# Other widths of query units in the second and third batch of a sketched-attention and expert-mixing kernel

## The chip, the cores and the metric

The kernel runs on one core of one Trainium2 chip. The time is the device time of one execution in microseconds (us); the median of four executions before the change is 489.26 us (489.24 to 489.73). TensorE multiplies matrices (PE in the profile; PEld are its weight loads), VectorE (DVE), ScalarE (ACT) and GpSimd (POOL) work on elements, and SyncE (SP) issues the DMA transfers. Each engine runs its instructions in the order in which the program emits them and waits on semaphores for the others.

## The reference

Two blocks follow each other. The first is attention without a softmax: queries and keys go through a product of two small projections (`phi`, 8 x 8 = 64 features), the keys of a batch are summed into one matrix per head, and each query row is multiplied with it and divided by its sum. The second mixes four experts: each is a two-layer network with a ReLU, weighted per row by a normalised gate.

```python
# q, k, v: (4, 4, 1088, 32); S1, S2: (8, 32)
def phi(x):
    a = np.einsum('rd,bhsd->bhsr', S1, x)
    b = np.einsum('rd,bhsd->bhsr', S2, x)
    return np.einsum('bhsi,bhsj->bhsij', a, b).reshape(*x.shape[:-1], 64)
q_p, k_p = phi(q), phi(k)
kv = np.einsum('bhsf,bhsd->bhfd', k_p, v)
z = np.sum(k_p, axis=2)
num = np.einsum('bhsf,bhfd->bhsd', q_p, kv)
den = np.einsum('bhsf,bhf->bhs', q_p, z)[..., None] + 1e-06
x = (num / den).transpose(0, 2, 1, 3).reshape(4352, 128)
# w1: (4, 128, 1024), w2: (4, 1024, 128)
p = domain_probs / (domain_probs.sum(-1, keepdims=True) + 1e-09)
out = sum(p[:, e:e+1] * (np.maximum(x @ w1[e], 0) @ w2[e]) for e in range(4))
```

## The kernel before

The 4352 rows of `x` are the columns of one SBUF tile `xT` (128 x 4352). Two streams of work share the engines.

The expert stream cuts the columns into eleven chunks, `CHUNKS = [128, 448, 512, 512, 512, 512, 512, 512, 320, 256, 128]`, counted here from 0. Chunk 3 begins at column 1088, chunk 4 at 1600, chunk 5 at 2112, chunk 6 at 2624, chunk 7 at 3136, chunk 8 at 3648. Each chunk takes 16 steps (`NQ`), one for each pair of 128-wide blocks of the hidden layer; "step 2.13" below is step 13 of chunk 2. A step runs `first(i)`: two groups of matmuls `h<-xT,w_sb` (j = 0 and 1), each followed by a ReLU on ACT (L807) and, on DVE, by one or two rectify-and-subtract operations (L778, three a step), and after each group a call of `work()`. Then it runs `second(i - 2)`: the matmuls `o<-hid` of the step two before. The `h` results rotate through three PSUM banks, so a group waits for the DVE and ACT readers of the group three before it. Every fourth step an expert is complete, and `gather` and `gather_rest` add it up on ACT and POOL.

The attention stream is a generator, `front()`, which makes `xT` batch by batch (1088 columns each): first `keys(b)`, then one `queries(b, c, n)` for each unit of `n` columns listed in `UNITS[b]`. It is cut into pieces by `yield`: 19 for the keys of a batch, 20 for a unit. Pieces of the keys: three transposes `kT`, three projections `kf`, eight products `kp` (DVE, L383), two empty ones, two `kv` sums on PE, one `kvx`. Pieces of a unit: the transpose `qT` (L480), two empty ones, the projection (`qc`, PE, `f<-qT,sq`), the shuffles and the addition `qf`, `qf`, `qb` (L629 to L634), twice `qa` (L639) with two products `qp` (L493), three empty ones, the attention matmuls (`den<-kvx,qp`), the reciprocal `rc` (L565, L570), the quotient `xs` (L574), and at last the transpose `y` (L583) with the stores: four DMAs put `y` into a DRAM buffer `xd` (L601) and a fifth brings it back as columns of `xT` (L609). Five DMAs a unit, all issued by SP.

How wide the unit is decides its tiles: `blocks(n)` gives ceil and floor of n/128. A unit of up to three tiles uses one PSUM bank, `den`; a fourth tile goes into a second bank, `num`, and `rc` and `xs` then have one instruction more each. Where the two numbers differ (320, 448), `qT` takes two transposes in place of one.

How many pieces a step carries is planned. `needed[m]` counts the pieces up to the end of the unit that completes the columns of chunk `m`. In each step the loop sets

```python
rate = CHUNKS[m] / NQ * max([0] + [(needed[c] + (8 if c > 1 else 4) - done[0]) / (START[c] - gone) for c in range(m + 1, NC)])
```

where `done[0]` counts pieces emitted and `gone` the columns already begun: the steepest line from now to eight pieces after each later chunk's need. Each `work()` adds half of `rate` to a credit and emits a piece for each whole credit. Pieces go into the engines' queues at that place: the DVE work of a piece stands between the L778 operations of the expert stream.

On SP the transfers stand in program order: the stores and the load of each unit, `load_gate(m + 1)` at step m.5, the output of chunk m - 1 at about step m.7, and `load_batch(b + 1)` (L93, L99, L104) after the keys of batch b.

Of the kernel before, what the change touches and what calls it, by code (L numbers as in the profile page):

```python
# [23 lines left out]
def kernel(  # L24
# [25 lines left out]
    P = 128  # L50
# [11 lines left out]
    CW = 512  # L62
    GE = 160
    LA = 2
    UNITS = [[P, 448, 512]] + [[384, 384, 320]] * 2 + [[384, 320, 384]]

    CHUNKS = [P, 448, 512] + [512] * 5 + [320, 256, P]
    NC = len(CHUNKS)
    START = [sum(CHUNKS[:m]) for m in range(NC)]
    assert all(sum(u) == S for u in UNITS) and sum(CHUNKS) == B * S  # L70

# [594 lines left out]
    def start():  # L666


        b, n = 0, UNITS[0][0]
        kf = []  # L670
# [39 lines left out]

        n1 = UNITS[b][1]
        qT = apool.tile([P, QW], F32, tag="qT2", name="qT2")
# [14 lines left out]
    def front():  # L727
        for b in range(B):
# [4 lines left out]
            c = 0  # L733
            for n in UNITS[b]:
                if b or c:
# [218 lines left out]

    needed, columns, count = [0] * NC, UNITS[0][0], 0
    for b in range(B):
        count += 19 if b else 0
        for n in UNITS[b] if b else UNITS[0][1:]:
            count, columns = count + (20 if count else 18), columns + n
# [76 lines left out]
```

## Time and profile before

| | |
|---|---|
| median of four executions | 489.26 us |
| the profiled execution | 489.73 us, of which the span is 487.9 us |
| PE busy | 482.2 us (99%) |
| DVE busy | 319.7 us (66%) |
| ACT busy | 247.0 us (51%) |
| POOL busy | 230.5 us (47%) |
| granted TensorE clock | 1.0 |

A line of the timeline begins with the start in us from the beginning of the span and the duration in us of a run of alike instructions; then come engine, line, operation, output and inputs, shapes and the number of instructions, and in brackets the idle time of the engine before it with what ended it. A `MATMUL` line counts instructions of which each 32-bit product takes two. A line of the view by stretches begins with the stretch; behind it stand its length and each engine's busy time in it with the number of instructions.

Chunk 1 begins at about 29 us, chunk 2 at 78.27, chunk 3 at 133.42, chunk 4 at 190.57, chunk 5 at 244.80, chunk 6 at 300.24, chunk 7 at 354.89, chunk 8 at 407.87 and chunk 9 at 442.22 us: the starts of the first `h` matmul of each.

### The profile page before, as it was taken

How to read it: one execution, taken by the hardware profiler on the slowest of the kernel's cores; microseconds unless marked ns; L12 is line 12 of the kernel's file. 1: busy time of each engine (PE TensorE's matmuls, PEld its weight loads, DVE VectorE, ACT ScalarE, POOL GpSimd, SP SyncE). 2: the span in 40 equal slices, each digit the busy share in tenths (PEclk: the TensorE clock that was granted, in tenths of full speed). 3: DMA queues.
4: the chain of work that ended last, by engine and by line, in shares of the span. 5: the costliest groups of instructions: out<-in, count | busy, mean ns of one | idle time of the engine just before them, and what ended most of it. 6: DMA issues, size and time to landing. Idle time of an engine off the chain costs nothing.

```text
span 487.9 us, 11354 instructions
## 1 busy us (share of the span) xinstructions
PE 482.2 (99%) x4543; PEld 367.5 (75%) x4543; DVE 319.7 (66%) x754; ACT 247.0 (51%) x496; POOL 230.5 (47%) x269
## 2 busy tenths in 40 slices
PE   8999999999999999999999999999999999999997
PEld 5966767677667777777777777777777777999996
DVE  6858685868766757768675674576574676665642
ACT  4354553445454634545455554545455455566751
POOL 5172653516345444424555354334555346565570
PEclk9999999999999999999999999999999999999999
DMA  8890230040102520041102200021101200120000
GB/s 241 256 305 5 90 93 2 12 126 1 35 1 91 129 55 1 1 118 24 34 0 87 50 2 2 1 86 24 34 0 56 50 1 0 45 53 6 15 3 18
DMA packets 37588, 26.25 MB, mean 54 GB/s; under 512 B 26016, under 2 KB 34592, under 8 KB 37024
## 3 DMA queue, kind: packets, MB, share of 16 engines
q1 hardware_dynamic: 37520, 25.53, 18.9%
q8 instruction: 36, 0.59, 0.5%
q14 instruction: 16, 0.13, 0.1%
q10 hardware_dynamic: 16, 0.00, 0.0%
HBM read 21.28 MB, written 4.24 MB: 52 GB/s over the span
## 4 chain that ended last, share of the span: by engine, by line
PE 72%; ACT 0%; DVE 0%; issue 0%
PE h L194 37%; PE o L194 31%; PE f L194 2%; PE den L194 2%; ACT sh L926 0%; PE num L194 0%; DVE end L846 0%
## 5 line engine op out<-in xcount | busy, mean ns | idle before, releaser
L194 PE MATMUL h<-xT,w_sb 128*64 128x512 f32 (+5 forms) x1432 | 299.4, 490 | 0.5 <-DVE hid L778 0.3
L778 DVE SCALAR_TENSOR_TENSOR hid<-h,hid 128x256 f32<-128x256 f32 (+6 forms) x432 | 203.9, 472 | 146.1 <-ACT hid L807 137.3
L807 ACT ACTIVATE hid<-h 128x512 f32<-128x512 f32 (+3 forms) x288 | 158.5, 551 | 194.3 <-PE h L194 154.3
L194 PE MATMUL o<-hid,w2s 128*64 128x256 f32 (+3 forms) x1152 | 222.9, 355 | 0.0
L194 PEld LDWEIGHTS h<-xT,w_sb 128*64 128x64 f32 x1432 | 147.9, 137 | 50.2 <-issue 5.8
L194 PE MATMUL o<-hid,w_sb 128*64 128x256 f32 (+3 forms) x864 | 183.8, 355 | 0.0
L194 PEld LDWEIGHTS o<-hid,w2s 128*64 128x64 f32 x1152 | 132.1, 137 | 29.2 <-issue 1.0
L922 POOL TENSOR_TENSOR ev<-yz,sh 64x256 f32<-64x256 f32 (+3 forms) x72 | 48.1, 668 | 161.7 <-ACT sh L925 159.0
L194 PEld LDWEIGHTS o<-hid,w_sb 128*64 128x64 f32 x864 | 100.7, 137 | 21.6 <-issue 3.4
L910 POOL TENSOR_TENSOR yz<-ev 128x512 f32<-128x512 f32 (+3 forms) x36 | 42.6, 1183 | 59.3 <-ACT ev L913 59.2
L922 POOL TENSOR_TENSOR ct<-ev 128x512 f32<-128x512 f32 (+3 forms) x36 | 42.4, 1178 | 2.8
L922 POOL TENSOR_TENSOR total<-total,ct 128x512 f32<-128x512 f32 (+3 forms) x27 | 32.3, 1195 | 2.1
L922 POOL TENSOR_TENSOR ct<-ct,gate 128x512 f32<-128x512 f32 (+3 forms) x27 | 32.2, 1191 | 2.1
L493 DVE TENSOR_TENSOR qp<-qa,qb 64x384 f32<-64x384 f32 (+3 forms) x44 | 30.4, 691 | 1.1
L912 ACT COPY ev<-o 128x512 f32<-128x512 f32 (+3 forms) x36 | 19.4, 539 | 11.9 <-PE o L194 11.5
L194 PE MATMUL o<-w_sb,hid 128*64 128x128 f32 x256 | 21.3, 274 | 0.0
L913 ACT COPY ev<-o 128x512 f32<-128x512 f32 (+3 forms) x36 | 19.4, 539 | 2.3 <-PE o L194 0.4
L194 PEld LDWEIGHTS o<-w_sb,hid 128*64 128x64 f32 x256 | 16.9, 137 | 1.8 <-issue 0.9
L799 ACT ACTIVATE hid<-h 128x256 f32<-128x256 f32 x24 | 8.8, 385 | 18.2 <-PE h L194 17.8
L383 DVE TENSOR_TENSOR kp<-fs 128x256 f32<-128x256 f32 (+1 forms) x24 | 15.0, 633 | 0.1
L194 PEld LDWEIGHTS den<-kvx,qp 128*64 128x64 f32 x264 | 13.0, 137 | 2.4 <-issue 0.5
L925 ACT COPY sh<-yz 64x256 f32<-64x256 f32 (+3 forms) x36 | 13.7, 380 | 1.7 <-POOL yz L910 0.8
(126 smaller groups left out, 239.5 us busy)
## 6 DMA issues: line engine op xcount, KB each, us to landing
w_sb<-in_moe_w_dram SPq DMA_DIRECT2D x8, 512.0 KB, 7.7
gate<-gates SPq DMA_DIRECT2D x4, 1024.0 KB, 4.7
kn<-in_k_dram SPq DMA_DIRECT2D x4, 544.0 KB, 4.3
vn<-in_v_dram SPq DMA_DIRECT2D x16, 128.0 KB, 4.5
gate<-gates SPq DMA_DIRECT2D x2, 896.0 KB, 4.5
qn<-in_q_dram SPq DMA_DIRECT2D x3, 544.0 KB, 5.7
xd<-y SPq DMA_DIRECT2D x26, 48.0 KB, 1.7
out_dram<-ob SPq DMA_DIRECT2D x16, 64.0 KB, 2.1
```

The lines of the kernel that those rows point to most:

```text
L194: nc.tensor.matmul(out(s), weights(s), moving(s), **flags)
L383: eng.tensor_tensor(out=_ap(kps[b], 0, P, 256 * t0 + P * p + 64 * x, [[256, n], [32, 2], [R, 4], [1, R]]), in0=_ap(src, 0, P, off + 4 * x, ...
L493: nc.vector.tensor_tensor(out=qp[p][64 * x : 64 * x + 64, 0:n], in0=qa[64 * p : 64 * p + 64, 0:n], in1=qb[64 * p : 64 * p + 64, 0:n], op=A ...
L778: nc.vector.scalar_tensor_tensor(out=out, in0=src, scalar=0.0, in1=in1, op0=ALU.max, op1=ALU.subtract)
L799: nc.scalar.activation(hd[:, 0 : 2 * n], hp[:, 0 : 2 * n], ACTF.Relu)
L807: nc.scalar.activation(hd[:, n * j : n * j + n], hp[:, 0:n], ACTF.Relu)
L910: add = lambda out, in0, in1, op=ALU.add: nc.gpsimd.tensor_tensor(out=out, in0=in0, in1=in1, op=op)
L912: nc.scalar.copy(_ap(ev, 0, P, 0, [[2 * w, 2], [1, w]]), _ap(a0, 0, P, 0, two))
L913: nc.scalar.copy(_ap(ev, 0, P, w, [[2 * w, 2], [1, w]]), _ap(a1, 0, P, 0, two))
L922: add = lambda out, in0, in1, op=ALU.add: nc.gpsimd.tensor_tensor(out=out, in0=in0, in1=in1, op=op)
L925: nc.scalar.copy(sh[HP:P, 0:w], yz[0:HP, 0, 0:w])
```

## The change

One constant is different. Batch 0 and batch 3 keep their units; in batch 1 the units 384, 384, 320 become 512, 320, 256, in batch 2 they become 448, 512, 128.

```diff
-    UNITS = [[P, 448, 512]] + [[384, 384, 320]] * 2 + [[384, 320, 384]]
+    UNITS = [[P, 448, 512], [512, 320, 256], [448, 512, P], [384, 320, 384]]
```

The ends of the units in columns of `xT` move from 1472, 1856, 2176 to 1600, 1920, 2176 in batch 1 and from 2560, 2944, 3264 to 2624, 3136, 3264 in batch 2. The number of pieces in all stays 275. With the rule for `needed` this gives, for chunks 0 to 10:

```
before  0 18 38 97 117 176 196 235 255 275 275
after   0 18 38 77 117 156 176 235 255 275 275
```

## The prediction

> **What bounds the kernel now.** I read the busy times and the chain that ended last, then the view by stretches for the places where PE is not full, then the timeline there, SP's lines included.
>
> ```profile
> PE 482.2 (99%) x4543; PEld 367.5 (75%) x4543; DVE 319.7 (66%) x754; ACT 247.0 (51%) x496; POOL 230.5 (47%) x269
> ...
> PE 72%; ACT 0%; DVE 0%; issue 0%
> ```
>
> ```profile
> 48.00:60.00 12.00, 12.00 (x135) 9.50 (x135) 8.06 (x21) 6.38 (x13) 6.55 (x8) 1.00 0.27 84
> 60.00:72.00 12.00, 11.71 (x92) 7.53 (x90) 9.21 (x18) 7.41 (x16) 7.36 (x9) 1.00 0.34 102
> ...
> 132.00:144.00 12.00, 11.79 (x82) 6.96 (x80) 9.23 (x23) 5.84 (x11) 7.05 (x6) 1.00 0.04 14
> 144.00:156.00 12.00, 12.00 (x108) 8.80 (x106) 7.59 (x17) 6.49 (x12) 6.54 (x6) 1.00 0.07 16
> ```
>
> PE (the first pair of numbers behind the comma) is full. Behind the start-up (24 us) only two of the twelve-us stretches ahead of the last one are short of 12.00, so the change can win only what these two lack, and can lose by making a third. "Busy" is generous, because the modelled end of a matmul hides a short gap; I take the size of a stall from the spacing of starts. Undisturbed, two steps of a 512 chunk take 6.45 us (the chain has h groups at 187.51 and 193.96), alternately 3.27 and 3.19.
>
> ```profile
> 67.24 1.05 DVE L383 TENSOR_TENSOR kp<-fs 128x256 f32<-128x256 f32 x1
> ...
> 69.42 1.45 DVE L383 TENSOR_TENSOR kp<-fs 128x320 f32<-128x320 f32 x1
> ...
> 70.79 0.38 DVE L778 SCALAR_TENSOR_TENSOR hid<-h,hid 128x224 f32<-128x224 f32 x1
> ...
> 71.22 0.97 PE L194 MATMUL h<-xT,w_sb 128*64 128x448 f32 x4 [0.29 <-DVE hid L778]
> ```
>
> The first stall, in step 1.14. The h group at 71.22 waits for the L778 that ends at 71.17, and that one stood behind products of batch 1's keys of 1.05 and 1.45 us, where the unhindered ones take 0.56; POOL worked from 65.3 to 72.8 almost without a pause. Steps 1.13 and 1.14 begin at 67.00 and 69.67, step 1.15 at 73.16: 6.16 us for a pair that takes 5.66 one pair earlier (61.34 to 67.00), 0.50 too much. Steps 1.14 and 1.15 together (69.67 to 78.27) take 8.60, less 5.66, less 2.10 for the 72 `kv` matmuls (steps 3.11 and 3.12, which carry as many, take 8.55 and not 6.45): 0.84. First stall: 0.50 to 0.84.
>
> ```profile
> 124.94 0.57 DVE L583 STREAM_TRANSPOSE y<-xs 128x384 f32<-128x384 f32 x1
> ```
>
> ```profile
> 125.54 1.73 SPq L601 DMA_DIRECT2D xd<-y  x4
> 130.83 0.34 SPq L609 DMA_DIRECT2D xT<-xd  x1
> ...
> 133.42 1.94 PE L194 MATMUL h<-xT,w_sb 128*64 128x512 f32 x8 [0.21 <-ACT sh L926]
> ...
> 341.10 1.74 SPq L601 DMA_DIRECT2D xd<-y  x4
> 344.21 0.34 SPq L609 DMA_DIRECT2D xT<-xd  x1
> ```
>
> The second stall is the beginning of chunk 3. The bracket names an ACT copy, which this matmul doesn't read; what it reads and what comes last is `xT`, whose columns from 1472 on belong to the unit stored at 125.54. Their load was issued only at 130.83, and with the 2.3 us that such a load takes it lands at 133.1. Step 2.15 begins at 129.60 and carries no matmul of the other stream, so chunk 3 should begin at 132.87: 0.55 us. From store to use this transfer took 7.9 us; at 341.10 the load came 2.2 us sooner behind the stores.
>
> **The change part by part.** PE: the tiles per batch are 3+3+3 before, 4+3+2 and 4+4+1 after, nine each; the projections cover 1088 columns a batch either way. The instruction counts of PE, ACT, POOL and SP stay. Nothing, and it needs no cover.
>
> DVE: a 384 unit costs, by its rows, qT 0.56, qf 0.59 + 0.55, qb 0.59, qa 2 x 0.585, qp 4 x 0.75, rc 0.39, xs 0.55, y 0.57: 8.0 us. A 512 unit: 0.67, 0.74 + 0.68, 0.73, 2 x 0.73, 4 x 0.78, rc 0.57, xs 0.55 + 0.28, y 0.71: 9.5. A 320 unit 6.9. For 256 and 128 the shuffles have no row; those for 512 and 320 (0.735, 0.515) fall 0.22 over 192 columns, which puts them near 0.44 and 0.29. With the 128x256 and 128x128 rows of the rest these units come to 5.8 and 3.8, a 448 unit to 8.8. Batch 1: 22.9 before, 22.2 after; batch 2: 22.9 and 22.1. The six extra instructions (three rc at 0.16, three xs at 0.28) are in that. DVE is idle a third of the span, so its total is worth nothing; its places count.
>
> The plan: with `needed` of chunk 3 at 77 and not 97, the steepest line is flatter. Following the loop, pieces per step go from 2.6 to 2.1 in chunk 1, 3.0 to 2.4 in chunk 2, 2.5 to 2.4 in chunks 3 and 4, and from 1.85 up to 2.4 in 5 and 6; chunk 7 keeps 1.5.
>
> First stall. The eight `kp` move from steps 1.11-1.13 to 1.12-2.0 and get four steps, not 2.75. A 448 step lasts 2.83 us, of which L778 takes 1.4, so 1.25 steps more give DVE 1.8 us, over twice the stall. But POOL's stretch now meets about four of the eight. At 1.1 us each (blocked ones took 0.88, 1.05, 1.45) steps 1.12 to 1.14 need some 1.5 us more than they last, against a cover of 1.4 (in step 1.11 an L778 ends at 63.35 whose bank is written again at 64.77). Up to 0.3 may remain. Gain 0.3 to 0.84; I take 0.6, the middle, since four steps are nearer to the quiet rows of batch 3 (no wait).
>
> Second stall. Chunk 3's columns now end with the first unit of batch 1, whose `y` falls in step 2.10 instead of 2.13: five steps of at least 3.2 us, 16, against 7.9. Gain 0.55, with 8 us to spare. Likewise chunk 4 (y in 3.11, 14 us ahead), chunk 5 (4.11, 13) and chunk 6 (5.3, 40).
>
> The transfer that becomes tighter is chunk 7's: batch 3's first unit stores in the second half of step 6.12, before in the first half of 6.11. There `y` follows the step's own L778 and ends 4.4 us after the step's start (338.25 to 342.04 in step 6.11, and 0.57 of `y`). Four steps and a projection, 13.5 us, lead to chunk 7. 9.1 us remain for 7.9 at worst: nothing, cover 1.2. SP's queue ahead is empty by then (gate load in 6.5, output in 6.7).
>
> DVE elsewhere. The densest `kp` are now those of batch 3 (5.15 to 6.2) and batch 2 (3.14 to 4.1), three in one step with POOL busy, as in 3.9 before; there the next h group still had 0.7 us. Wide `qp` stand in 2.6-2.7, 4.7-4.8 and 4.15-5.1. Per four steps: nine pieces of 6.7 us, 6.1 of L778, 0.7 of an output transpose, 13.5 in 12.9: a lag of 0.6 against a cover of 1.7 (an L778 ends at 111.31, its bank is written again at 113.02). Held up by POOL, `qp` of 384 columns took 0.88 to 1.58 against 0.57; one more of these is covered, two at once cost some 0.5. I take 0, with 0.5 to lose in the range.
>
> The 128-column unit stores runs of 128 bytes. The row of this size (16 KB, 1.5 us to landing) is no slower than that of 48 KB (1.7). Its columns (3136 to 3264) are stored in step 5.12 and read 20 steps later: nothing. The Trainium skill, "DMA: Bandwidth & Descriptors", Specifications, speaks against such units: below 512 bytes a transfer falls into read-modify-write. Were the landing doubled by that, an estimate from the page, the sum would be the same.
>
> Sum: 0.6 + 0.55 = 1.15 us off. The profiled execution would go from 489.73 to 488.6; its fellows lie 0.48 below it, and from the median 489.26 this gives **488.1 us**.
>
> **The rivals.** *A wait takes the place of a removed one.* Wide `qp` meet POOL twice in a step, or part of the first stall stays: 0.3 to 0.8 is given back. For it: the held-up `qp` of 1.53 and 1.58. Against it: each such case before ended with 0.65 us of cover or more. 488.1 + 0.55 = 488.65.
>
> *The plan moves, the stalls stay.* The first follows POOL's stretch and not the rate, and chunk 3 began late by something else than its load. Against it: the load's landing fits the gap to 0.3 us. 489.2.
>
> *Slower: DVE becomes the bound of the wide units.* Place: the three units with four tiles. At a mean piece of 0.74 us the lag is 0.6; from 0.87 on it passes the cover. If POOL holds up every `qp` there to 1.2, nine pieces take 4 x 1.2 + 3.6 = 8.4, the lag is 2.3 and each unit stalls PE by 0.6; the keys of batch 3 (eight at 1.2, 9.6, and 6.1 of L778 in 12.9) add 1.1. 2.9 in all, and if nothing is won at the two old places, where the same POOL works, 489.26 + 2.9 = 492.2; it decides from 1.0 on. Against it: only three of the eight `qp` in chunk 2 were held up.
>
> **How the numbers follow.** The forecast has 0.62 (its own range 487.8 to 488.4), the wait in place of the other 0.22, the stalls that stay 0.08, the slower rival 0.08. 0.2% is 0.98 us, about what a measurement of this kernel tells from no change: faster means below 488.28, slower above 490.24. The forecast lies by that edge, four fifths of it below: 0.50. Slower 0.08, the rest 0.42. The low end, 487.8, is both stalls at their upper bounds (1.39, 487.87); the high end, 489.1, holds the second case and leaves out most of the last two.
>
> **What would show it.** No wait of h on L778 near 70 us; chunk 2 beginning near 75.5, as the `kv` sums (2.1 us) move into it; chunk 3's first h 3.2 to 3.3 us after step 2.15's, or by a projection more, with the load of its columns issued 10 us before; PE at 12.00 in every stretch from 24 to 480 us. It is wrong if a stretch there falls short, above all near steps 2.7, 5.1 or 6.2, or if chunk 7's first h waits for a load.

## The result, and the profile after

The changed kernel takes 488.17 us (median of 38 runs, 487.76 to 488.95), the one before 489.06 us (58 runs, 488.73 to 490.37). The ratio is 0.9982, with a 95% interval of 0.9978 to 0.9987: 0.89 us faster. The interval does not reach 1, though single runs of the two kernels overlap; 0.89 us is a hair less than the 0.98 us that the prediction named as 0.2%. The median before has moved too: the four runs of the table stood at 489.26, and 489.73, the profiled one, is the second slowest of the 58. Two executions far from their fellows, 1821 us of the kernel of experiment 4 and 635.91 us (granted clock 0.753) of the kernel before, count in no ratio below.

The profiled execution of the changed kernel took 488.06 us, its span is 486.3 us. The busy times of its page, and the chain that ended last:

```profile
PE 481.5 (99%) x4543; PEld 362.7 (75%) x4543; DVE 321.1 (66%) x760; ACT 246.9 (51%) x496; POOL 229.8 (47%) x269
...
PE 97%; DMA 1%; DVE 1%; issue 0%; SPq 0%; ACT 0%; ACTq 0%
```

PE still sets the end, with the same 4543 instructions. The chain, which before ended at a wait at 133.42 us and held 72% of the span, now runs through to the start-up. The view by stretches (the first number behind the comma is PE's busy time in 12 us) at the two places of the prediction and at a third:

```profile
60.00:72.00 12.00, 12.00 (x117) 7.94 (x115) 8.06 (x18) 8.28 (x18) 6.62 (x7) 1.00 0.46 132
...
132.00:144.00 12.00, 12.00 (x104) 8.94 (x102) 7.30 (x17) 6.00 (x11) 5.84 (x5) 1.00 0.00 1
...
300.00:312.00 12.00, 12.00 (x140) 8.21 (x138) 9.65 (x18) 5.71 (x11) 5.80 (x6) 1.00 0.00 1
```

11.71 and 11.79 have become 12.00. The third line looks as full, and yet it holds a new wait of 0.26 us: this view cannot show one so short. The timeline of the changed kernel at three places (the first stall's, step 6.2 with POOL beside DVE, and SP before chunk 7):

```profile
68.72 0.94 DVE L383 TENSOR_TENSOR kp<-fs 128x256 f32<-128x256 f32 x1
69.47 1.67 PE L194 MATMUL h<-xT,w_sb 128*64 128x448 f32 x8
69.58 1.04 DVE L778 SCALAR_TENSOR_TENSOR hid<-h,hid 128x448 f32<-128x448 f32 x2
70.53 1.22 DVE L383 TENSOR_TENSOR kp<-fs 128x256 f32<-128x256 f32 x1
...
299.72 2.02 DVE L383 TENSOR_TENSOR kp<-fs 128x256 f32<-128x256 f32 x2
300.12 1.33 POOL L922 TENSOR_TENSOR ct<-ev 128x512 f32<-128x512 f32 x1
301.65 1.14 DVE L778 SCALAR_TENSOR_TENSOR hid<-h,hid 128x512 f32<-128x512 f32 x2
302.71 0.21 DVE L378 TENSOR_TENSOR fs<-num,fs 128x64 f32<-128x64 f32 x1
302.95 1.27 POOL L922 TENSOR_TENSOR total<-total,ct 128x512 f32<-128x512 f32 x1
302.96 1.61 DVE L383 TENSOR_TENSOR kp<-fs 128x320 f32<-128x320 f32 x1
304.49 0.41 DVE L778 SCALAR_TENSOR_TENSOR hid<-h,hid 128x256 f32<-128x256 f32 x1
...
344.34 1.74 SPq L601 DMA_DIRECT2D xd<-y  x4
347.44 0.34 SPq L609 DMA_DIRECT2D xT<-xd  x1
```

- Near 69 us a `kp` still takes 0.94 and 1.22 us, where one that begins with POOL idle takes 0.41 (at 71.98), but there are fewer of them in a step, and DVE is idle for 0.72 us in between (ahead of the L778 at 68.41, until an ACT result comes). The eight `h` matmuls of the step that begins at 69.47 run without a pause.
- Near 300 us two products come long (2.02 us for two, of which the second took 1.49, and 1.61 us for one). The L778 behind them ends at 304.90, and the second `h` group of step 6.2 starts at 304.95, 1.12 us after the first (303.84). Undisturbed the two are 0.86 us apart: 0.26 us lost. The matmul before it ends, as modelled, at about that time, so the view of waits does not list it either.
- Chunk 7's load is issued 3.1 us after its stores and lands at 350.67 us; the chunk begins at 353.32.

A sharper measure than busy time is a chunk's *excess*: the time from its first `h` matmul to the next chunk's, less its matmul columns at the pace at which undisturbed matmuls start (one of 512 columns every 0.42667 us on each half of the array: four of them begin within 1.28 us). For the chunks that differ, from the first trace of the kernel before, from a second one (the first experiment), and after:

| excess, us | chunk 1 | 2 | 3 | 6 | 1 to 7 |
|---|---|---|---|---|---|
| before, first trace | 1.59 | 1.09 | 0.75 | 0.63 | 5.85 |
| before, second trace | 1.58 | 0.54 | 0.73 | 0.63 | 5.28 |
| after | 0.52 | 0.73 | 0.53 | 0.92 | 4.48 |

The two halves of the array begin a chunk 0.01 to 0.37 us apart, and the measure follows the earlier one, so a tenth or two can pass from one chunk to the next. Against the second trace 0.80 us are won: 1.06 in chunk 1, of which about 0.2 only moves to chunk 2 with the 72 `kv` matmuls; 0.29 is given back in chunk 6; some 0.2 more is spread over chunk 3 and others in amounts that I can't assign. The whole way from chunk 1 to the last matmul is 454.65 us in the second trace and 453.87 after, 0.78 less. The second stall, 0.55 us in the first trace, is not there in the second, so the change cannot have won it there.

### The profile page after: what moved, and what is told of

Its sections match the earlier page's. It is cut to its first block, busy times and chain, and to the rows that moved or that the text cites. A ratio compares the mean times of both kernels' runs of the same rounds, so it can differ in the third digit from the quotient of the medians.

```text
span 486.3 us, 11359 instructions
## 1 busy us (share of the span) xinstructions
PE 481.5 (99%) x4543; PEld 362.7 (75%) x4543; DVE 321.1 (66%) x760; ACT 246.9 (51%) x496; POOL 229.8 (47%) x269
## 4 chain that ended last, share of the span: by engine, by line
PE 97%; DMA 1%; DVE 1%; issue 0%; SPq 0%; ACT 0%; ACTq 0%
PE h L194 50%; PE o L194 41%; PE f L194 3%; PE den L194 2%; DMA kn<-in_k_dram 1%; PE num L194 1%; DVE kp L383 0%; DVE qp L493 0%; DVE kT L320 0%; SPq L119 0%; DVE qT L480 0%; DVE end L846 0%; DVE kvz L406 0%; ACT fs L352 0%; ACT vx L329 0%
## 5 line engine op out<-in xcount | busy, mean ns | idle before, releaser
L778 DVE SCALAR_TENSOR_TENSOR hid<-h,hid 128x256 f32<-128x256 f32 (+6 forms) x432 | 203.8, 472 | 143.3 <-ACT hid L807 134.9
L493 DVE TENSOR_TENSOR qp<-qa,qb 64x512 f32<-64x512 f32 (+5 forms) x44 | 30.1, 685 | 1.0
L383 DVE TENSOR_TENSOR kp<-fs 128x256 f32<-128x256 f32 (+1 forms) x24 | 16.6, 697 | 0.1
L925 ACT COPY sh<-yz 64x256 f32<-64x256 f32 (+3 forms) x36 | 13.7, 381 | 1.7 <-POOL yz L910 0.8
L926 ACT COPY sh<-yz 64x256 f32<-64x256 f32 (+3 forms) x36 | 13.7, 381 | 0.9
```

The costliest lines, as they stand in the source:

```text
L383: eng.tensor_tensor(out=_ap(kps[b], 0, P, 256 * t0 + P * p + 64 * x, [[256, n], [32, 2], [R, 4], [1, R]]), in0=_ap(src, 0, P, off + 4 * x, ...
L493: nc.vector.tensor_tensor(out=qp[p][64 * x : 64 * x + 64, 0:n], in0=qa[64 * p : 64 * p + 64, 0:n], in1=qb[64 * p : 64 * p + 64, 0:n], op=A ...
L778: nc.vector.scalar_tensor_tensor(out=out, in0=src, scalar=0.0, in1=in1, op0=ALU.max, op1=ALU.subtract)
L925: nc.scalar.copy(sh[HP:P, 0:w], yz[0:HP, 0, 0:w])
L926: nc.scalar.copy(sh[0:HP, 0:w], yz[HP:P, 1, 0:w])
```

## The experiments

**1. The kernel before, once more.** No edit.

> The kernel before, unchanged, for a second trace: its profiled execution was 0.67 us above the median of 489.06. My theory (a DVE wait near 70 us in step 1.14, 0.5 to 0.8, and the load of chunk 3's columns coming late, 0.55): the first is there again at the same size, since it hangs on the order of instructions alone; the second hangs on how long a store takes to land and may be smaller. Rival (the first trace was an outlier and both waits are chance): neither is there, and the stretches 60-72 and 132-144 show PE at 12.00.

It took 489.05 us (span 487.3 us). From its view by stretches, and from the timeline of SP and of DVE:

```profile
60.00:72.00 12.00, 11.72 (x93) 7.46 (x91) 9.27 (x18) 7.40 (x16) 7.36 (x9) 1.00 0.35 102
132.00:144.00 12.00, 12.00 (x85) 8.62 (x83) 9.59 (x22) 6.06 (x12) 6.93 (x6) 1.00 0.01 1
```

```profile
69.35 1.44 DVE L383 TENSOR_TENSOR kp<-fs 128x320 f32<-128x320 f32 x1
...
125.47 1.73 SPq L601 DMA_DIRECT2D xd<-y  x4
128.54 0.34 SPq L609 DMA_DIRECT2D xT<-xd  x1
```

The first stall is the same to 0.01 us. The second is gone: the load follows the stores by 3.1 us, not 5.3, and chunk 3 begins at 132.79, 3.27 us after step 2.15, just what the prediction called undisturbed. What was late in the first trace is seen in the view of its transfers from 128.2 to 130 us (packets, MB, share):

```profile
q8 instruction: 1, 0.02, 3.1%
q14 instruction: 1, 0.01, 1.7%
q1 hardware_dynamic: 9, 0.00, 1.6%
```

A packet of 16 KB of the kind "instruction" begins at 128.67, one of 8 KB at 129.17, and the last nine packets of the four stores move only from 129.54 to 129.91. In the second trace the 16 KB packet came at 128.05, as the last packets of the stores were ending (128.09). The order is shown; that the one held up the others is what it suggests. Experiments 2 and 3b below leave this unit as it was and have no late load either: it is in one trace of four.

**2. POOL's work taken away at the first stall.** `gather_rest` leaves out the gate multiplication and the addition for expert 1 of chunk 1.

```diff
-        add(by_blocks(ct if e else total[m], n), by_blocks(ct, n), gate_of(m, e), ALU.mult)
-        if e:
+        if (m, e) != (1, 1):
+            add(by_blocks(ct if e else total[m], n), by_blocks(ct, n), gate_of(m, e), ALU.mult)
+        if e and (m, e) != (1, 1):
```

> The kernel before without the two GpSimd operations that apply the gate of expert 1 to chunk 1 and add it to the total (68.09 and 69.38 in the trace of before, 2.35 us of the stretch from 65.3 to 72.8); the output lacks that expert for these 448 columns. The pieces and their rate stay. My theory (the products kp are held up by POOL, and the rate leaves no room for that): the kp at 69.42 takes 0.7 and not 1.45, the h group near 71.2 waits for nothing, 0.5 to 0.8 below before: 488.2 to 488.5. Rival (the rate alone, 2.6 pieces, fills DVE): the wait stays at 0.3 or more, the time within 0.25 of 489.03.

488.41 us (11 runs) against 489.15 for the kernel before on the same chip, ratio 0.9989 (0.9978 to 0.9999). Its timeline, where POOL is now idle from 68.98 for 1.95 us:

```profile
68.07 0.91 POOL L663 TENSOR_TENSOR w2s<-w_sb,w2s 128x256 f32<-128x256 f32 x1
69.51 0.49 DVE L383 TENSOR_TENSOR kp<-fs 128x320 f32<-128x320 f32 x1
70.12 1.67 PE L194 MATMUL h<-xT,w_sb 128*64 128x448 f32 x7
70.93 1.14 POOL L910 TENSOR_TENSOR yz<-ev 128x448 f32<-128x448 f32 x1 [1.95 <-ACT ev L913]
```

In the first trace of the kernel before, this instruction of POOL, the addition that is left out here, was running when the `kp` of 69.42 began; it ended at 70.52, and the `kp` 0.35 us later, at 70.87:

```profile
69.38 1.14 POOL L922 TENSOR_TENSOR total<-total,ct 128x448 f32<-128x448 f32 x1
```

The same `kp` now takes 0.49 us instead of 1.44, and `h` does not wait. Chunk 1's excess falls from 1.58 to 0.74 us; 0.09 of that comes back in chunk 2, and from chunk 1 to the last matmul 0.75 us are won. So the first stall is POOL holding up a DVE product, and its size is 0.75 to 0.84 us, at the upper of the two bounds that the prediction gave.

**3. Each batch alone.** (a) only batch 1, (b) only batch 2 with the new widths:

```diff
+    UNITS = [[P, 448, 512], [512, 320, 256], [384, 384, 320], [384, 320, 384]]
```
```diff
+    UNITS = [[P, 448, 512], [384, 384, 320], [448, 512, P], [384, 320, 384]]
```

> Batch 1 alone gets 512, 320, 256. Chunk 3 then needs 77 pieces but chunk 5 still 176, so chunk 1 carries 2.36 pieces a step and chunk 2 2.7. My theory: the second wait goes whole; of the first, which meets POOL at a rate between 2.1 and 2.6, half stays: 488.3 to 488.6. Rival (the plan has to be flat over both batches): no gain, 489.06.

> Batch 2 alone gets 448, 512, 128. Chunks 1 to 3 keep their pieces as before, 2.6, 3.0 and 2.5 a step; only 4 to 6 change, to 2.2 each. My theory: both waits stay, nothing is won: 489.06 within 0.15. Rival (what is won lies in chunks 4 to 6): 488.6 or less.

(a) 488.56 us, ratio 0.9988 (0.9979 to 0.9997); (b) 489.04 us, ratio 1.0007 (0.9998 to 1.0016), both beside 489.03. In (b) the `h` group of step 1.14 waits as before. In (a) the stall is smaller and one step later:

```profile
70.83 2.26 DVE L383 TENSOR_TENSOR kp<-fs 128x320 f32<-128x320 f32 x2
73.01 0.38 DVE L778 SCALAR_TENSOR_TENSOR hid<-h,hid 128x224 f32<-128x224 f32 x1
```

Two `kp` of 2.26 us stand ahead of the L778 that `h` needs, and `h` starts at 73.45; chunk 1's excess is 0.76 us. Batch 1 alone wins half, batch 2 alone nothing, both together 0.89: batch 2's widths lower `needed` of chunk 5, the steepest line becomes flatter still, and the products are spread further. Between the traces of (a) and of the whole change the excess falls by 0.24 us in chunk 1 and 0.13 in chunk 2, long before batch 2 itself is worked on, and by 0.19 in chunk 3; 0.09 is given back in chunk 4 and 0.29 in chunk 6. That is 0.21 of the 0.39 us between the medians; where the rest is, these traces don't show.

**4. The new widths with the old plan.** The changed kernel with the counts of before written behind the loop that makes them:

```diff
+    needed = [0, 18, 38, 97, 117, 176, 196, 235, 255, 275, 275]
```

> The new widths with the needs of the old plan, 0 18 38 97 117 176 196 235 255 275 275, written in: the pieces stand as before the change, but chunk 3's columns end with the first unit of batch 1. My theory: the second wait goes, the first stays, as kp stands in 1.11-1.13 at 2.6 pieces: 0.3 to 0.55 below before, 488.5 to 488.8. Rival A (the flatter plan does all): as before, 489.06. Rival B (the widths do all): as the changed kernel, 488.17.

489.41 us (11 runs), ratio 1.0005 (0.9996 to 1.0014): nothing is left of the gain. My expectation was too low, since it still gave the widths part of it. A second run of this kernel, for a trace, asked where the rest is:

> The kernel of e2 once more, for a trace: its median was 489.41, not the 488.5 to 488.8 that I expected. Since e1 shows that the second wait was chance, nothing is left to win here but 0; and the 0.35 on top should be a new wait: the first one stays near 71 us as in e1, and wide pieces at 3.0 a step run DVE out of its cover once more, in steps 2.3 to 2.5 or 2.9 to 2.11. Rival (0.35 is scatter): no wait of h on DVE but the one near 71 us.

It took 489.23 us. The first stall is there (chunk 1's excess 1.59 us), and chunk 2 has 0.86 against 0.54. The size was as I thought, the mechanism was not: the least cover of an `h` group in chunk 2 is 0.38 us (step 2.5), so none of them waits for DVE. In step 2.7 it is the projection that waits:

```profile
102.90 0.70 DVE L583 STREAM_TRANSPOSE y<-xs 128x512 f32<-128x512 f32 x1
103.52 0.53 DVE L480 STREAM_TRANSPOSE qT<-qn 128x192 f32<-128x192 f32 x2
104.11 0.76 PE L194 MATMUL f<-qT,sq 128*64 128x320 f32 x4
```

`f` needs `qT`, which stands behind the wide `y` and ends at 104.05: about 0.15 us. As much goes in step 2.12, for a reason that I did not find. By this trace the wide units are a small loss by themselves (0.32 us, all in chunk 2), which the times alone can't tell from none; the counts are what wins.

**5. The old widths with the new plan.**

```diff
+    needed = [0, 18, 38, 77, 117, 156, 176, 235, 255, 275, 275]
```

> The old widths with the needs of the changed kernel, 77, 156 and 176 for chunks 3, 5 and 6, written in: the flatter rates without the units that end with the chunks. The columns of chunk 3 and of chunk 5 are then not made when these chunks begin, and the loop emits the missing 8 and 6 pieces at once in front of the first h of the chunk. My theory (the widths are needed so that the plan can be flat): PE waits twice for a chain of these DVE pieces and a store and load, 8 to 12 us each, 505 to 513 in all. Rival (the flat rate alone wins): 488.2 to 488.6.

510.51 us in one execution (span 508.7 us). With the old widths the columns of chunks 3 and 5 end in the second unit of their batch, so at 77 or 156 pieces they are not made; the step loop then emits what is missing (8 and 6 pieces) all at once, and PE waits for it and for the transfer. Its timeline at chunk 3, and three stretches (in the view by stretches the granted clock is the third number from the end):

```profile
130.62 0.59 PE L194 MATMUL o<-hid,w2s 128*64 128x256 f32 x2
...
140.97 3.68 PE L194 MATMUL h<-xT,w_sb 128*64 128x512 f32 x8 [7.26 <-issue]
```

```profile
132.00:141.00 9.00, 1.18 (x26) 0.93 (x27) 2.58 (x6) 0.00 (x0) 4.65 (x4) 0.67 0.19 45
141.00:147.00 6.00, 6.00 (x26) 2.66 (x28) 2.02 (x5) 1.19 (x2) 0.00 (x0) 0.65 0.00 0
147.00:150.10 3.10, 3.10 (x25) 2.05 (x23) 0.88 (x2) 1.42 (x3) 0.00 (x0) 1.00 0.00 0
```

The two places cost 11.6 us (9.5 in the wait and its step, 2.1 behind it) and 10.7 us (7.9 and 2.8). The sum, 22.3, less what chunk 1 wins, explains the 21.4 us of slowdown: chunk 1's excess is 0.52 us here, as after the change, 1.06 below before. So the flatter counts take the first stall away with the old widths too. But a flat plan is no free choice: it needs widths that end where the chunks end, and that is what the change buys.

**6. The same keys, a little earlier.** If the 0.26 us in step 6.2 is two held-up `kp` in one step, moving batch 3's keys should free it. The changed kernel with twelve pieces ahead of chunk 7's need, not eight:

```diff
-(needed[c] + (8 if c > 1 else 4) - done[0])
+(needed[c] + (12 if c == 7 else 8 if c > 1 else 4) - done[0])
```

> The changed kernel with a margin of 12 pieces in place of 8 for chunk 7: the rate goes from 2.4 to 2.5 and the keys of batch 3 stand a step earlier, kp in 5.14 to 6.1 and not 5.15 to 6.2, so that three and not five meet POOL's stretch of 6.0 and 6.1. My theory: the wait of the changed kernel in step 6.2 (0.26) goes and none comes: 487.9. Rival (any denser plan makes another wait of that size): 488.2 or more.

487.91 us (8 runs), ratio to the kernel before 0.9975 (0.9965 to 0.9985). In the timeline around 301 us:

```profile
300.13 1.11 DVE L383 TENSOR_TENSOR kp<-fs 128x320 f32<-128x320 f32 x1
...
303.05 0.42 DVE L778 SCALAR_TENSOR_TENSOR hid<-h,hid 128x256 f32<-128x256 f32 x1 [0.33 <-ACT hid L807]
```

DVE waits for ACT there, where it was late before; chunk 6's excess is 0.72 us, down from 0.92. The larger margin also raises the rate of the chunks ahead of it a little; chunk 5's excess falls from 0.67 to 0.56 us. To compare it with the changed kernel itself, both ran on one chip:

> The changed kernel, unchanged, beside e10 on the same chip. My theory: 0.7 to 1.0 below before, and the wait in step 6.2 is there again at 0.2 to 0.3, since it hangs on the order of instructions. Rival (the wait in 6.2 was chance like the late load): no h group waits on DVE near 305 us.

> The kernel of e8 once more, against e9 on the same chip. My theory: 0.2 to 0.3 below e9, by the wait in step 6.2 that it lacks. Rival (e8 drew a good chip): within 0.1 of e9.

The changed kernel: 488.12 us (487.89 to 488.54, 11 runs), ratio 0.9980 (0.9971 to 0.9989); its trace has the long `kp` again (1.60 us at 302.86) and the same wait in step 6.2. With earlier keys: 487.75 us (487.60 to 488.07, 7 runs), ratio 0.9974 (0.9963 to 0.9984). The difference, 0.37 us, is somewhat over the expected 0.2 to 0.3; the two traces put 0.31 of it at chunks 1 to 7, 0.20 in chunk 6. By its median this version is the fastest of the three, though its slowest run (488.07) overlaps the changed kernel's fastest (487.89).

## Why the prediction was right, step by step

The time, 488.17 for 488.1 us, was right. The two terms that made it, 0.6 + 0.55, were not: one was too small, one was not there, and a third, taken as 0, was a loss. So the hit is in part luck: the median of four that I began from stood 0.20 us above that of the 58, my sum was 0.26 us more than the 0.89 measured, and the two nearly cancel.

- **"First stall … I take 0.6."** The mechanism held: a product of the keys held up by POOL stands ahead of an L778 (experiment 2), and the flatter plan spreads the products (3 and 4). The size was at the upper bound, 0.75 to 0.84, and the stall went whole; the "up to 0.3" did not remain. The 0.56 us that I gave an unhindered product is the mean of its group, held-up ones included: with no POOL instruction running it takes 0.41 at 256 columns and 0.48 at 320. I had let every meeting with POOL count as delay in a step, but DVE had 0.72 us of idle time between them.
- **"Second stall … Gain 0.55."** This is the step that failed. The wait was real in its one execution, and the reason that I gave, a load issued late behind its stores, was right there. But it is not part of the kernel's ordinary time: four traces with that placement have it once. That the profiled execution stood 0.48 us over its fellows, nearly the stall, should have been a warning. I subtracted the stall from the median, which mostly did not contain it. Only the span of the first trace (487.9 to 486.3, 1.6 us) shows both gains.
- **"I take 0, with 0.5 to lose."** Of that 0.26 us came, in step 6.2, one of the three places named, by products of batch 3's keys meeting POOL (experiment 6 shows it a second time, and its absence with earlier keys). The analogue that I leaned on, step 3.9, had 0.68 us of cover left behind products of 0.98 and 1.32 us, 1.4 more than undisturbed; here three of 0.60, 1.49 and 1.61 took 2.4 more.
- **DVE's total.** The widths' rows summed to 1.5 us less; measured is 1.4 more than in the first trace before and 0.2 more than in the second (320.9 us), so two executions of one kernel differ here by nearly as much as I summed. `kp`, which I left out since its count does not change, went from 15.0 to 16.7 us behind the start-up, because POOL holds its instructions up for longer: ten of 24, nine before. It cost nothing that shows except in step 6.2.
- **Chunk 7's transfer.** `y` should end 4.4 us behind the start of step 6.12 and 9.1 us remain; it was 4.44 and 9.0, with the load landed 2.6 us before its use. The 128-column unit delayed nothing that the trace shows: its last two stores landed 1.5 us after their issue, as predicted, and not twice that.
- **The marks to look for.** No wait of `h` on L778 near 70 us, chunk 2 at 75.12 for 75.5, chunk 3's first `h` 3.19 us behind step 2.15's with its load issued 11.9 us ahead: all came. "PE at 12.00 in every stretch" came too, and hid the new wait; the spacing of the starts showed it.
- **The rivals.** A wait in place of a removed one happened at about half of its price (0.26 for 0.55). That the stalls stay is refuted for the first. DVE as the bound of the wide units did not come: no L778 in chunk 2 made `h` wait, even with the old plan at 3.0 pieces a step (4), and the 0.3 us lost there went another way.

So the sum of the ordinary executions reads 0.75 won at the first stall, 0.26 lost in step 6.2, and some 0.3 won that is spread thinly and has no shown cause: 0.80 between the traces, against 0.89 measured.

## What to carry to other kernels

A gain is to be summed from waits that every trace has: a second profile of the unchanged kernel costs little and would have struck out half of this sum. Where one stream is dealt out between another's steps, the widths of its units matter by where they end against the other's chunks, because that sets how flat the dealing can be; the widths alone bought nothing, and the flat plan without them cost 21 us. Waits of a few tenths of a microsecond on a pipelined engine are found by the spacing of its starts, not by its busy share.

## What was not expected of the hardware

**A pause of PE costs more than its length.** In experiment 5, PE stood idle for 7.3 us; the granted clock is 0.67 in that stretch, 0.65 in the next 6 us, and 1.00 again from 147.0 on. The first step behind the pause took 5.18 us instead of 3.2, that at chunk 5 5.93, so some 2 and 2.7 us are added to the waits. The Trainium skill, "TensorE: Matmul & The Clock Gate", in "HAM oscillation — how this bites in real kernels", says that gaps of PE of more than about 3.4 us bring the throttle back, so that the next work begins cold. This trace agrees, with 7.3 us of gap; the stalls of 0.26 to 0.84 us in the other runs stand in stretches at 1.00, and no trace here has a pause behind the start-up between 0.92 and 7.3 us.

**A DVE product that ends with POOL's instruction.** The `kp` of 128x320 takes 0.47 to 0.49 us where no POOL instruction is running when it begins, 0.83 in experiment 2 (at 71.58), 1.44 to 1.45 before and 1.61 after. How busy POOL is does not decide this: the one at 304.82 after takes 0.48 us although POOL works through 0.7 of it. What decides is the POOL instruction that is already running when the product begins. Over eleven traces, whenever that instruction still had more than 0.2 us to run, the product ended 0.35 us behind it (0.345 to 0.354, 57 cases), and the one of 128x256 0.28 us behind it (0.278 to 0.287, 46 cases); a POOL instruction that began later added nothing. The traces list no wait of the one for the other. Leaving out two POOL operations gave 0.74 us of the kernel's time.

**Transfers that no line of the kernel issues.** Packets of the kind "instruction", 36 of 16 KB and 16 of 8 KB in the span, stand beside the kernel's own in the view of transfers. Where one came ahead of the last nine packets of a group of stores, these ended about 1.75 us later than in the other trace; that it held them up is not shown.
